# Attention scores computed head by head over 64 array rows, in alternating halves, with pooled keys transposed without zero blocks

## The chip, the core and the metric

The kernel runs on one core of a Trainium2 chip. TensorE (PE in the profile; PEld are its weight loads) does the matrix products, VectorE is DVE, ScalarE is ACT, GpSimd is POOL, and SyncE is SP, which issues the transfers here. The metric is device microseconds of one execution.

## The reference: what is computed

Pooled attention feeds two blocks of dense products. Only the first part is touched by the change. q, k and v have 8 batches, 8 heads, 576 positions and a head width of 64.

```
k_p = k.reshape(B, H, Sp, pool, D).mean(axis=3)       # 576 keys pooled by 8: 72 keys
v_p = v.reshape(B, H, Sp, pool, D).mean(axis=3)
scores = scale * np.matmul(q, k_p.transpose(0, 1, 3, 2))
...
attn = np.exp(scores)
attn = attn / (np.sum(attn, axis=-1, keepdims=True) + 1e-09)
return np.matmul(attn, v_p).astype(np.float32)
...
x = _moe_ref(x=x, **moe_kwargs)        # x @ w_in, softmax-gated, normed, @ w_out
return _moe2_ref(x=x, **moe2_kwargs)   # ((x @ w1) * (x @ w2) @ w3) @ w_out
```

## The kernel before, in words

The work has three stretches. In the first some 145 us the first weights are loaded and converted while attention starts. Up to about 585 us attention and the first dense block run interleaved on PE in slots. From there on the rest of the first block and the second block follow, without attention.

PE and SP follow an order that is written out by hand: each step is `put` into a numbered slot, and the steps of a slot are emitted one after the other, together with a piece of the dense products (`HEAVY`: h is L567, x is L624 to L626). The order on DVE, ACT and POOL in these stretches is set by a scheduler.

Attention works on 16 groups, two for each of the 8 batches; a group has two query tiles of 128 rows, and every second group a third tile of 64, so that there are 40 tiles. For each tile `pq` transposes the queries of the 8 heads, two heads (a pair) at a time, and ACT copies them to `qT`: its 128 rows are two heads of 64. `sc` (L436) computes the scores in two PSUM banks. `exp` takes the maxima on DVE (L454) and the exponentials of 72 keys a head on ACT (L457), `normalize` divides on POOL (L477, L484), `pt` transposes the result, and `av` multiplies it with the pooled values (L539); ACT and DVE copy that away (`split`, L100 and L101, and X, L543).

Three PSUM banks (`bank`, tag "ba", `bufs=3`) are shared in rotation by pq, the two halves of sc, pt, av and the transposed keys (pkm, pkl), so that a step that opens a bank waits until its user three openings earlier has been read.

A batch's pooled keys come into `bdt`, 128 rows by 4 pairs by 2 by 72: for a pair, the two heads' keys stand on the diagonal and zeros elsewhere. One matmul of 128 rows and 144 columns thus gives a pair's scores. The zeros come with the transposes: `pool_k` sums the keys on DVE (L324), ACT spreads the sums into a zeroed `KBD` (L327), and `transpose_k` transposes its four blocks (L358). The last 8 pooled keys (`pool_kl`) are multiplied with a mask into `KLB` on POOL (L346), transposed (L362) and copied by DVE (L368). For the first batch PE itself does the pooling (`pool_k_first`, L340).

An f32 matmul of the program stands in the trace as two weight loads and two matmuls, so a tile's four score matmuls are eight rows of L436. A transpose is one of each, and so are the products of type fp32r.

Of the kernel before, what the change touches and what calls it, by code (L numbers as in the profile page):

```python
# [8 lines left out]
F32 = mybir.dt.float32  # L9
# [3 lines left out]
AF = mybir.ActivationFunctionType  # L13
ALU = mybir.AluOpType
# [4 lines left out]
def attention_moe_kernel(  # L19
# [53 lines left out]
    def bank(name):  # L73
        return PS.tile([P, 512], F32, tag="ba", name=name, bufs=3)
# [7 lines left out]
    ident = const.tile([P, P], F32, tag="ident", name="ident")  # L82
# [50 lines left out]
    def after(d, fn, *args, first=3):  # L133
        put(now + d, fn, *args, first=first)
# [7 lines left out]
    A1 = att.enter_context(tc.tile_pool(name="att1", bufs=1, side="right"))  # L142
    A = att.enter_context(tc.tile_pool(name="att", bufs=2, side="right"))
# [7 lines left out]
    class Rounded:  # L151
        def __init__(self, w, i):
            self.w, self.i = w, i
# [116 lines left out]
    QL = A1.tile([P, H, D], F32, tag="QL", name="QL")  # L270
    KLB = A1.tile([P, H, D], F32, tag="KLB", name="KLB")
    nc.gpsimd.memset(QL, 0.0)
    nc.gpsimd.memset(KLB, 0.0)

    def heads(t, n):
        return t.rearrange("p (o d) -> p o d", o=1).to_broadcast([n, H, D])

    def head_mask(n):
        return mask8[0:n].rearrange("p (h o) -> p h o", o=1).to_broadcast([n, H, D])

    def tree(t, n):

        for w in (4, 2, 1):
            nc.gpsimd.tensor_tensor(t[..., 0 : w * n], t[..., 0 : w * n], t[..., w * n : 2 * w * n], ALU.add)

    class Batch:


        def __init__(self, b):
            self.b = b  # L290
            self.k, self.v = [None, None], [None, None]

        def load_main(self, src, to, i):
            t = A.tile([P, 2, POOL * D], F32, tag="kvn", name=f"kv{self.b}_{i}")
            for hh in range(2):
                nc.sync.dma_start(
                    t[64 * hh : 64 * hh + 64],
                    src[self.b, 4 * i + hh : 4 * i + hh + 3 : 2, 0:512, :].rearrange("h (k e) d -> k h (e d)", e=POOL),
                )
            to[i] = t  # L300

        def load_left(self, src, copies):
            t = A.tile([P, POOL * D], F32, tag="kvl", name=f"kvl{self.b}", bufs=1)
            for c in range(copies):
                nc.sync.dma_start(
                    t[64 * c : 64 * c + 64], src[self.b, :, 512:S, :].rearrange("h (k e) d -> h k (e d)", e=POOL)
                )
            return t

        def load_k(self, i):  # L310
            self.load_main(k, self.k, i)

        def load_kl(self):
            self.kl = self.load_left(k, 1)

        def load_v(self, i):
            self.load_main(v, self.v, i)

        def load_vl(self):
            self.vn = self.load_left(v, 2)  # L320

        def pool_k(self, i):
            kp = A.tile([P, 2, D], F32, tag="kp", name=f"kp{self.b}_{i}", bufs=1)
            nc.vector.tensor_reduce(kp, self.k[i].rearrange("p c (e d) -> p c d e", e=POOL), axis=AX.X, op=ALU.add)  # L324
            for hh in range(2):
                r = slice(64 * hh, 64 * hh + 64)
                nc.scalar.activation(KBD[r, 2 * i : 2 * i + 2, hh, :], kp[r], AF.Copy)  # L327

        def pool_k_first(self, i):

            if i == 0:
                self.pm = bank(f"pkm{self.b}")
                self.bdt = A.tile([P, NP, 2, KP], F32, tag="bdt", name=f"bdt{self.b}")
                nc.gpsimd.memset(self.bdt, 0.0)
            for c in range(2):
                for a in range(2):
                    r, o = slice(D * a, D * a + D), (2 * i + c) * P + D * a
                    for e in range(POOL):
                        s_ = self.k[i][:, c, e * D : e * D + D]
                        nc.tensor.matmul(  # L340
                            self.pm[r, o : o + D], s_, ident[:, r], start=(e == 0), stop=(e == POOL - 1)
                        )

        def pool_kl(self):
            tree(self.kl[0:64], D)
            nc.gpsimd.tensor_tensor(KLB[0:64], heads(self.kl[0:64, 0:D], 64), head_mask(64), ALU.mult)  # L346

        def transpose_k(self):
            if self.b == 0:
                bdt, pm = self.bdt, self.pm.rearrange("p (c a k) -> p c a k", c=NP, a=2)  # L350
                for a in range(2):
                    r = slice(D * a, D * a + D)
                    nc.scalar.activation(bdt[r, :, a, 0:KM], pm[r, :, a, :], AF.Copy)
            else:
                bdt = self.bdt = A.tile([P, NP, 2, KP], F32, tag="bdt", name=f"bdt{self.b}")
                pm = bank(f"pkm{self.b}")
                for p in range(NP):
                    nc.tensor.transpose(pm[:, p * P : p * P + P], KBD[:, p].rearrange("p a d -> p (a d)"), ident)  # L358
                nc.scalar.activation(bdt[:, :, :, 0:KM], pm.rearrange("p (c a k) -> p c a k", c=NP, a=2), AF.Copy)
            pl = bank(f"pkl{self.b}")  # L360
            for p in range(NP):
                nc.tensor.transpose(  # L362
                    pl[:, p * P : p * P + P], KLB[:, 2 * p : 2 * p + 2].rearrange("p a d -> p (a d)"), ident
                )

            def left():
                for p in range(NP):
                    nc.vector.tensor_copy(  # L368
                        bdt[:, p, :, KM:KP],
                        pl[:, p * P + 16 * p : p * P + 16 * p + 16].rearrange("p (a k) -> p a k", a=2),  # L370
                    )

            after(1, left)
# [21 lines left out]
    class Group:  # L395
# [32 lines left out]

        def sc(self, t):
            n, nm = P, f"{self.a}_{t}"  # L430
            qT, bdt = self.st[t], self.batch.bdt
            half = []
            for a in range(2):
# [9 lines left out]
                half.append(sc[0:n, 0 : 4 * KP].rearrange("p (h k) -> p h k", h=4))  # L443
            self.st[t] = half
            after(self.gaps[0], self.exp, t, first=6)

        def exp(self, t):
            n, nm, half = P, f"{self.a}_{t}", self.st[t]
            mx = A.tile([P, H], F32, tag="mx", name="mx" + nm)
            sm = A.tile([P, H], F32, tag="sm", name="sm" + nm)  # L450
            e = A.tile([P, H, KP], F32, tag="ea", name="ea" + nm)
            for a in range(2):
                hs = slice(4 * a, 4 * a + 4)
                nc.vector.tensor_reduce(mx[0:n, hs], half[a], axis=AX.X, op=ALU.max, negate=True)  # L454
                for h in range(4):
                    x = 4 * a + h
                    nc.scalar.activation(  # L457
                        e[0:n, x],
                        half[a][:, h],
                        AF.Exp,  # L460
                        bias=mx[0:n, x : x + 1],
                        scale=1.0,
                        accum_out=sm[0:n, x : x + 1],
                    )
            self.st[t] = e, sm
            after(self.gaps[1], self.normalize, t)
# [243 lines left out]
    for un in units:  # L710
        s_ = SLOTS * un.u
# [49 lines left out]
    with tc.manual_schedule(engines={mybir.EngineType.PE, mybir.EngineType.SP}):  # L761
        for s_ in range(min(events), SLOTS * (NU + 1) + 2):
# [3 lines left out]
            u, c = s_ // SLOTS, s_ % SLOTS  # L766
            kind, n = HEAVY[c], c % 4
# [82 lines left out]
    for m in range(FC):  # L850
# [6 lines left out]
        if m in BLOCKS_AT:  # L857
            i = BLOCKS_AT.index(m)
# [206 lines left out]
```

## Time and profile before

| | |
|---|---|
| median of 3 runs | 1326.9 us (1325.52 to 1329.15) |
| the profiled execution | 1330.36 us, its span 1328.6 us |
| PE busy over the span | 1240.8 us (93%) |
| DVE, ACT, POOL busy | 820.4, 535.9, 421.8 us |
| mean granted PE clock | 0.976 |

Busy time of PE holds the pipelined end of each matmul, so that the pace of a stretch is read from the starts of neighbouring rows and not from the durations.

### The profile page before, as it was taken

How to read it: one execution, taken by the hardware profiler on the slowest of the kernel's cores; microseconds unless marked ns; L12 is line 12 of the kernel's file. 1: busy time of each engine (PE TensorE's matmuls, PEld its weight loads, DVE VectorE, ACT ScalarE, POOL GpSimd, SP SyncE). 2: the span in 40 equal slices, each digit the busy share in tenths (PEclk: the TensorE clock that was granted, in tenths of full speed). 3: DMA queues.
4: the chain of work that ended last, by engine and by line, in shares of the span. 5: the costliest groups of instructions: out<-in, count | busy, mean ns of one | idle time of the engine just before them, and what ended most of it. 6: DMA issues, size and time to landing. Idle time of an engine off the chain costs nothing.

```text
span 1328.6 us, 21980 instructions
## 1 busy us (share of the span) xinstructions
PE 1240.8 (93%) x8284; PEld 1128.1 (85%) x8284; DVE 820.4 (62%) x1627; ACT 535.9 (40%) x1517; POOL 421.8 (32%) x509
## 2 busy tenths in 40 slices
PE   6777999999998999999999999999999999999992
PEld 5466888888888888898898899999999999999992
DVE  4989777777877777644348555545554645454541
ACT  5465666566665656554345222212121212121210
POOL 3433434253434434220000142424242433334220
PEclk8879999999999999999999999999999999999996
DMA  9533445453535464313124101020101101010000
GB/s 233 136 79 104 135 128 159 123 143 116 153 113 140 120 167 120 100 48 126 52 91 153 32 2 64 1 64 1 64 10 55 46 19 64 1 64 1 33 1 32
DMA packets 85698, 109.43 MB, mean 82 GB/s; under 512 B 43608, under 2 KB 43608, under 8 KB 85592
## 3 DMA queue, kind: packets, MB, share of 16 engines
q1 hardware_dynamic: 85592, 108.03, 28.3%
q8 instruction: 65, 1.06, 0.3%
q14 instruction: 41, 0.34, 0.1%
HBM read 78.65 MB, written 29.36 MB: 81 GB/s over the span
## 4 chain that ended last, share of the span: by engine, by line
PE 73%; DVE 11%; DMA 6%; ACT 3%; issue 3%; POOL 1%; SPq 1%; ACTq 0%; DVEq 0%; POOLq 0%
PE p L925 9%; PE p L927 9%; PE p L926 9%; PE h L567 8%; PE acc L971 5%; PE acc L974 5%; PE acc L973 5%; DMA f<-in_moe_w_dram 4%; PE x L625 4%; PE x L626 4%; PE x L624 4%; PE sc L436 2%; PE av L539 2%; PE lt L610 1%; DVE kp L324 1%
## 5 line engine op out<-in xcount | busy, mean ns | idle before, releaser
L945 POOL TENSOR_TENSOR a<-a,b 128x256 f32<-128x256 f32 x72 | 53.0, 736 | 479.4 <-DVE b L944 351.0
L929 ACT ACTIVATE p<-p 128x256 f32<-128x256 f32 x72 | 27.9, 387 | 397.2 <-PE p L927 365.3
L625 PE MATMUL x<-lnl,gwh 128*128 128x256 f32 x576 | 164.1, 285 | 4.1 <-DVE lnl L614 4.0
L624 PE MATMUL x<-lnh,gwh 128*128 128x256 f32 x576 | 167.2, 290 | 0.0
L626 PE MATMUL x<-lnh,gwl 128*128 128x256 f32 x576 | 163.4, 284 | 0.0
L189 POOL TENSOR_TENSOR cvb<-cvb,cvm 128x512 f32<-128x512 f32 x46 | 60.1, 1306 | 212.4 <-DVE cvm L182 159.9
L625 PEld LDWEIGHTS x<-lnl,gwh 128*128 128x128 f32 x576 | 110.7, 192 | 6.1 <-DVE lnl L614 5.2
L974 PE MATMUL acc<-wfl,ph 128*128 128x512 f32 x288 | 113.1, 393 | 0.0
L457 ACT ACTIVATE ea<-sc,mx 128x72 f32<-128x72 f32 x320 | 98.4, 329 | 36.1 <-DVE mx L454 35.9
L973 PE MATMUL acc<-wfh,ph 128*128 128x512 f32 x288 | 112.9, 392 | 0.0
L624 PEld LDWEIGHTS x<-lnh,gwh 128*128 128x128 f32 x576 | 110.6, 192 | 1.2 <-ACT lnh L613 0.2
L626 PEld LDWEIGHTS x<-lnh,gwl 128*128 128x128 f32 x576 | 110.7, 192 | 0.0
L944 DVE TENSOR_TENSOR b<-b,p 128x256 f32<-128x256 f32 x72 | 30.2, 420 | 123.0 <-PE p L927 123.0
L567 PE MATMUL h<-winh,xh 128*128 128x512 f32 x288 | 100.4, 430 | 0.0
L567 PE MATMUL h<-winl,xh 128*128 128x512 f32 x288 | 91.3, 399 | 0.0
L567 PE MATMUL h<-winh,xl 128*128 128x512 f32 x288 | 90.3, 395 | 0.0
L614 DVE TENSOR_TENSOR lnl<-lt,lnh 128x512 fp32r<-128x512 f32 x72 | 49.3, 687 | 55.6 <-ACT lnh L613 55.2
L925 PE MATMUL p<-th,w1h 128*128 128x256 f32 x288 | 81.6, 283 | 1.1 <-ACT p L929 1.1
L971 PE MATMUL acc<-wfh,pl 128*128 128x512 f32 x288 | 82.6, 393 | 0.0
L926 PE MATMUL p<-th,w1h 128*128 128x256 f32 x288 | 81.5, 283 | 0.0
L927 PE MATMUL p<-th,w1l 128*128 128x256 f32 x288 | 81.5, 283 | 0.0
L933 DVE TENSOR_TENSOR u<-p,p 128x256 f32<-128x256 f32 x72 | 30.4, 422 | 77.3 <-PE p L927 77.3
(196 smaller groups left out, 3766.0 us busy)
## 6 DMA issues: line engine op xcount, KB each, us to landing
f<-in_moe_w_dram SPq DMA_DIRECT2D x32, 512.0 KB, 6.2
x2d<-xo SPq DMA_DIRECT2D x36, 256.0 KB, 2.0
xq<-x2d SPq DMA_DIRECT2D x36, 256.0 KB, 2.8
out_dram<-ot SPq DMA_DIRECT2D x36, 256.0 KB, 2.6
kv<-in_k_dram SPq DMA_DIRECT2D x32, 256.0 KB, 3.8
q<-in_q_dram SPq DMA_DIRECT2D x32, 256.0 KB, 7.0
kv<-in_v_dram SPq DMA_DIRECT2D x32, 256.0 KB, 3.7
f<-in_moe_w_out_dram SPq DMA_DIRECT2D x16, 512.0 KB, 5.8
```

The source lines that it names most:

```text
L189: self.engine.tensor_tensor(self.f, self.f, self.m.bitcast(F32), ALU.add)
L457: nc.scalar.activation(e[0:n, x], half[a][:, h], AF.Exp, bias=mx[0:n, x : x + 1], scale=1.0, accum_out=sm[0:n, x : x + 1],)
L567: nc.tensor.matmul(self.ph[:, a], s_[:, c], w_[:, c, a * 512 : a * 512 + 512], start=first, stop=last)
L624: nc.tensor.matmul(o, gw[0][:, f, ws], self.th[:, f], start=(f == 0), stop=False)
L625: nc.tensor.matmul(o, gw[0][:, f, ws], self.tl[:, f], start=False, stop=False)
L626: nc.tensor.matmul(o, gw[1][:, f, ws], self.th[:, f], start=False, stop=(f == FC - 1))
L925: nc.tensor.matmul(o, wh[:, c, fsl], th[:, c], start=c == 0, stop=False)
L926: nc.tensor.matmul(o, wh[:, c, fsl], tl[:, c], start=False, stop=False)
L927: nc.tensor.matmul(o, wl[:, c, fsl], th[:, c], start=False, stop=c == 1)
L971: nc.tensor.matmul(accs[t], pl[:, ts], wh, start=False, stop=(fc == FC - 1))
L973: nc.tensor.matmul(accs[t], ph[:, ts], wh, start=(fc == 0), stop=False)
L974: nc.tensor.matmul(accs[t], ph[:, ts], wl, start=False, stop=False)
```

## The change

The keys of a batch come into one of two tiles `KT`, 128 rows by 4 pairs by 72, with no zeros: the upper 64 rows hold one head of a pair and the lower 64 the other. `sc` does one matmul for each head, 64 rows by 72 columns, alternately for the first head of a pair (rows 0 to 63, first bank) and the second (rows 64 to 127, second bank). The heads of a bank are therefore every second one, and `exp` writes them to their places.

The keys are loaded in another arrangement of heads, so that the pooled sums of two heads stand side by side in `kp`, which is transposed as it is: two transposes in place of four, without KBD and ACT's copies into it. The last 8 keys are summed by POOL into two equal blocks of columns, transposed by one matmul over 64 rows, and copied by two DVE copies in place of four. For the first batch PE pools with 128 moving columns and half as many matmuls. `kl` and `vl` have buffers of their own. Three fills on POOL (KBD, KLB, and `bdt` for the first batch) and the mask product are gone.

```diff
-    KBD = A1.tile([P, NP, 2, D], F32, tag="KBD", name="KBD")
+    KT = [A1.tile([P, NP, KP], F32, tag=f"kt{i}", name=f"kt{i}") for i in range(2)]
-    nc.gpsimd.memset(KBD, 0.0)
-    nc.gpsimd.memset(KLB, 0.0)
...
         def pool_k(self, i):
-            kp = A.tile([P, 2, D], F32, tag="kp", name=f"kp{self.b}_{i}", bufs=1)
+            kp = self.kp[i] = A.tile([P, 2, D], F32, tag="kp", name=f"kp{self.b}_{i}")
             nc.vector.tensor_reduce(kp, self.k[i].rearrange("p c (e d) -> p c d e", e=POOL), axis=AX.X, op=ALU.add)
-            for hh in range(2):
-                r = slice(64 * hh, 64 * hh + 64)
-                nc.scalar.activation(KBD[r, 2 * i : 2 * i + 2, hh, :], kp[r], AF.Copy)
...
         def pool_kl(self):
-            tree(self.kl[0:64], D)
-            nc.gpsimd.tensor_tensor(KLB[0:64], heads(self.kl[0:64, 0:D], 64), head_mask(64), ALU.mult)
+            t = self.kl[0:64]
+            for w in (4, 2):
+                nc.gpsimd.tensor_tensor(t[:, 0 : w * D], t[:, 0 : w * D], t[:, w * D : 2 * w * D], ALU.add)
+
+            for c in (2, 3):
+                nc.gpsimd.tensor_tensor(t[:, c * D : c * D + D], t[:, 0:D], t[:, D : 2 * D], ALU.add)
...
+            if self.b:
+                self.pm = bank(f"pkm{self.b}")
+                for i in range(2):
+                    nc.tensor.transpose(
+                        self.pm[:, i * P : i * P + P], self.kp[i].rearrange("p a d -> p (a d)"), ident
+                    )
+            kt, pm = self.kt, self.pm[:, 0 : NP * KM].rearrange("p (c k) -> p c k", c=NP)
+
+            pl = bank(f"pkl{self.b}")[:, 0:64]
+            nc.tensor.transpose(pl, self.kl[0:64, 2 * D : 4 * D], ident[0:64, 0:64])
+            nc.scalar.activation(kt[:, :, 0:KM], pm, AF.Copy)
...
-            half = []
-            for a in range(2):
-                sc = bank(f"sc{nm}_{a}")
-                for p in range(2):
+            sc = [bank(f"sc{nm}_{a}") for a in range(2)]
+            for p in range(NP):
+                for a in range(2):
+                    r = slice(D * a, D * a + D)
                     nc.tensor.matmul(
-                        sc[0:n, p * 2 * KP : p * 2 * KP + 2 * KP],
-                        qT[:, 2 * a + p, 0:n],
-                        bdt[:, 2 * a + p].rearrange("p a k -> p (a k)"),
-                        start=True,
-                        stop=True,
+                        sc[a][0:n, p * KP : p * KP + KP], qT[r, p, 0:n], kt[r, p], start=True, stop=True
                     )
```

On PE, at the second tile of an odd group, behind `av` and ahead of the x products, this stood before (x2 counts the two pairs of a half; sc_1_0 and sc_1_1 are the two banks):

```order
L539 MATMUL av_3_3397<-ptx_3029,VLL 128x320
L436 MATMUL sc_1_0_3412<-bdt_3183,qT_1_3344 128x144 x2
L436 MATMUL sc_1_1_3415<-bdt_3183,qT_1_3344 128x144 x2
L624 MATMUL x_5_1_3421<-lnh_3080,gwh 128x256
L625 MATMUL x_5_1_3421<-lnl_3081,gwh 128x256
```

And this stands there in the changed kernel (the line numbers are its own; a row is one matmul of the program):

```order
L532 MATMUL av_3_3391<-ptx_3025,VLL 128x320
L434 MATMUL sc_1_0_3406<-kt_105,qT_1_3338 128x72
L434 MATMUL sc_1_1_3407<-kt_105,qT_1_3338 128x72
L434 MATMUL sc_1_0_3406<-kt_105,qT_1_3338 128x72
L434 MATMUL sc_1_1_3407<-kt_105,qT_1_3338 128x72
L434 MATMUL sc_1_0_3406<-kt_105,qT_1_3338 128x72
L434 MATMUL sc_1_1_3407<-kt_105,qT_1_3338 128x72
L434 MATMUL sc_1_0_3406<-kt_105,qT_1_3338 128x72
L434 MATMUL sc_1_1_3407<-kt_105,qT_1_3338 128x72
L617 MATMUL x_5_1_3419<-lnh_3074,gwh 128x256
```

The second bank, which the third matmul of a tile opened before, is now opened by the second matmul of eight; the steps around it are the same.

On DVE, at the same tile, the queue was this before (mx are the two maxima of the tile, one for each bank; xl and X read the banks of av, VBDl are the values of the next batch, ST and e belong to h):

```order
L575 TENSOR_REDUCE ST<-h_1_3312 128x1
L101 TENSOR_TENSOR xl_3353<-av_2_3388,xh_3352 128x256
L543 COPY X_98<-av_2_3388 128x64
L101 TENSOR_TENSOR VBDl<-kv_1_3103,VBDh 64x2x64
L454 TENSOR_REDUCE mx_1_3439<-sc_1_0_3412 128x4
L101 TENSOR_TENSOR VBDl<-kv_1_3103,VBDh 64x2x64
L582 SCALAR_TENSOR_TENSOR e_1_3385,ST<-h_1_3312,e_1_3385 128x1024
L101 TENSOR_TENSOR xl_3353<-av_3_3397,xh_3352 128x256
L543 COPY X_98<-av_3_3397 128x64
L454 TENSOR_REDUCE mx_1_3439<-sc_1_1_3415 128x4
```

In the changed kernel it is this:

```order
L568 TENSOR_REDUCE ST<-h_1_3306 128x1
L101 TENSOR_TENSOR xl_3347<-av_2_3382,xh_3346 128x256
L536 COPY X_98<-av_2_3382 128x64
L101 TENSOR_TENSOR VBDl<-kv_1_3101,VBDh 64x2x64 x2
L180 SCALAR_TENSOR_TENSOR cvb<-f_3366,cvb 128x512
L575 SCALAR_TENSOR_TENSOR e_1_3379,ST<-h_1_3306,e_1_3379 128x1024
L101 TENSOR_TENSOR xl_3347<-av_3_3391,xh_3346 128x256
L536 COPY X_98<-av_3_3391 128x64
L447 TENSOR_REDUCE mx_1_3437<-sc_1_0_3406 128x4
L447 TENSOR_REDUCE mx_1_3437<-sc_1_1_3407 128x4
```

The first maximum has moved behind a weight conversion (cvb), e, xl and X; both maxima now stand together.

On ACT, at the start of the program, the rows up to the first queries were these before:

```order
L170 ACTIVATE cvm<-f_133 128x512
L353 ACTIVATE bdt_164<-pkm_163 64x4x64 x2
L204 ACTIVATE winh<-cvb 128x512
L424 ACTIVATE qT_0_274<-pq_0_269 128x512
L170 ACTIVATE cvm<-f_137 128x512
```

In the changed kernel they are these:

```order
L170 ACTIVATE cvm<-f_131 128x512
L361 ACTIVATE kt_105<-pkm_161 128x4x64
L421 ACTIVATE qT_0_232<-pq_0_227 128x512
L204 ACTIVATE winh<-cvb 128x512
L170 ACTIVATE cvm<-f_135 128x512
```

The queries' copy qT has moved ahead of a weight copy (winh), and the keys take one copy in place of two.

## Rows read from the trace of the kernel before

**Rows 1.** The page: span, and busy time of each engine.

```profile
span 1328.6 us, 21980 instructions
PE 1240.8 (93%) x8284; PEld 1128.1 (85%) x8284; DVE 820.4 (62%) x1627; ACT 535.9 (40%) x1517; POOL 421.8 (32%) x509
```

**Rows 2.** Busy time by stretch (length, engines, granted clock, DMA share, GB/s).

```profile
0.00:145.00 145.00, 107.65 (x604) 85.01 (x604) 115.39 (x230) 74.97 (x244) 60.08 (x83) 0.88 0.55 141
145.00:585.00 440.00, 418.50 (x2863) 383.90 (x2864) 324.15 (x642) 275.49 (x930) 168.79 (x217) 0.99 0.47 128
```

**Rows 3.** Who PE waited for, 145 to 585 us: total, times, longest.

```profile
PE av L539 <- DVE xl L101: 8.5, 5, 1.9
PE sc L436 <- DVE X L543: 7.1, 6, 1.4
...
PE sc L436 <- DVE xl L101: 1.5, 4, 0.4
```

**Rows 4.** The score line, 145 to 585 us: ns min/median/max, first and last start.

```profile
L436 PEld LDWEIGHTS sc<-bdt,qT x248: 186/190/337, 149.9 to 568.4; 128*128 128x128 f32 x124
L436 PE MATMUL sc<-bdt,qT x248: 283/286/607, 150.0 to 568.6; 128*128 128x144 f32 x124
```

**Rows 5.** One tile's scores: in the chain (start, us), and on PE's timeline after idling.

```profile
491.98 0.98 PE sc L436 x8
...
101.61 1.25 PE L436 MATMUL sc<-bdt,qT 128*128 128x144 f32 x8 [0.69 <-ACT qT L424]
102.69 0.49 PE L610 MATMUL lt<-ident,e 128*128 128x128 f32 x3
```

**Rows 6.** A tile that waits for its second bank, timelines of PE and DVE.

```profile
384.98 0.65 PE L436 MATMUL sc<-bdt,qT 128*128 128x144 f32 x4
386.69 0.73 PE L436 MATMUL sc<-bdt,qT 128*128 128x144 f32 x4 [1.06 <-DVE X L543]
...
386.34 0.21 DVE L543 COPY X<-av 128x64 f32<-128x64 f32 x1
```

**Rows 7.** PE's timeline where matmuls use 64 of the array's columns, and leave them.

```profile
12.73 1.15 PE L340 MATMUL pkm<-ident,kv 128*64 128x64 f32 x20
...
15.41 0.46 PE L340 MATMUL pkm<-ident,kv 128*64 128x64 f32 x5
15.79 0.66 PE L362 MATMUL pkl<-ident,KLB 128*128 128x128 f32 x4
16.28 0.60 PE L421 MATMUL pq<-ident,q 128*128 128x128 f32 x4
```

**Rows 8.** L340 by shape, 13 to 15.5 us: busy us, mean ns.

```profile
L340 PE MATMUL pkm<-ident,kv 128*64 128x64 f32 x56 | 2.9, 225 | 0.0
L340 PEld LDWEIGHTS pkm<-ident,kv 128*64 128x64 f32 x54 | 2.7, 138 | 0.0
```

**Rows 9.** PE's timeline at four transposes that run back to back.

```profile
290.44 0.60 PE L610 MATMUL lt<-ident,e 128*128 128x128 f32 x4
290.87 1.15 PE L436 MATMUL sc<-bdt,qT 128*128 128x144 f32 x8
```

**Rows 10.** ACT's copies into KBD: by line, and what ACT waited for (0 to 590 us).

```profile
L327 ACT ACTIVATE KBD<-kp 64x128 f32<-64x128 f32 x28 | 8.6, 309 | 26.8 <-DVE kp L324 26.6
...
ACT KBD L327 <- DVE kp L324: 26.6, 14, 3.1
```

**Rows 11.** ACT's and PE's timeline at the first scores.

```profile
15.96 0.77 ACT L353 ACTIVATE bdt<-pkm 64x256 f32<-64x256 f32 x2 [1.83 <-PE pkm L340]
16.75 0.63 ACT L204 ACTIVATE winh<-cvb 128x512 fp32r<-128x512 f32 x1
17.41 0.60 ACT L424 ACTIVATE qT<-pq 128x512 f32<-128x512 f32 x1
...
18.06 0.64 PE L436 MATMUL sc<-bdt,qT 128*128 128x144 f32 x3 [1.17 <-ACT qT L424]
```

**Rows 12.** From the tile of rows 6 on: its normalization on POOL, its transposes on PE.

```profile
394.17 0.55 POOL L484 TENSOR_TENSOR pr<-ea,sm 128x64 f32<-128x64 f32 x2
...
397.63 0.60 PE L502 MATMUL pt<-ident,pr 128*128 128x128 f32 x4
398.07 0.27 PE L505 MATMUL px<-ident,pr 128*128 128x128 f32 x1
```

More of the change, by code (lines that the diff above doesn't have):

```diff
@@ L290, in __init__, with load_main, load_left @@
             self.b = b
-            self.k, self.v = [None, None], [None, None]
-        def load_main(self, src, to, i):
+            self.k, self.v, self.kp = [None, None], [None, None], [None, None]
+            self.kt = KT[b % 2]
+        def load_main(self, src, to, i, heads_of):
             t = A.tile([P, 2, POOL * D], F32, tag="kvn", name=f"kv{self.b}_{i}")
-            for hh in range(2):
+            for r in range(2):
                 nc.sync.dma_start(
-                    t[64 * hh : 64 * hh + 64],
-                    src[self.b, 4 * i + hh : 4 * i + hh + 3 : 2, 0:512, :].rearrange("h (k e) d -> k h (e d)", e=POOL),
+                    t[64 * r : 64 * r + 64],
+                    src[self.b, heads_of(4 * i, r), 0:512, :].rearrange("h (k e) d -> k h (e d)", e=POOL),
                 )
             to[i] = t
-        def load_left(self, src, copies):
-            t = A.tile([P, POOL * D], F32, tag="kvl", name=f"kvl{self.b}", bufs=1)
+        def load_left(self, src, copies, tag):
+            t = A.tile([P, POOL * D], F32, tag=tag, name=f"{tag}{self.b}", bufs=1)
             for c in range(copies):
@@ L310, in load_k @@
         def load_k(self, i):
-            self.load_main(k, self.k, i)
+            self.load_main(k, self.k, i, lambda h, r: slice(h + 2 * r, h + 2 * r + 2))
         def load_kl(self):
-            self.kl = self.load_left(k, 1)
+            self.kl = self.load_left(k, 1, "kl")
         def load_v(self, i):
-            self.load_main(v, self.v, i)
+            self.load_main(v, self.v, i, lambda h, r: slice(h + r, h + r + 3, 2))
         def load_vl(self):
-            self.vn = self.load_left(v, 2)
+            self.vn = self.load_left(v, 2, "vl")
         def pool_k(self, i):
-            kp = A.tile([P, 2, D], F32, tag="kp", name=f"kp{self.b}_{i}", bufs=1)
+            kp = self.kp[i] = A.tile([P, 2, D], F32, tag="kp", name=f"kp{self.b}_{i}")
             nc.vector.tensor_reduce(kp, self.k[i].rearrange("p c (e d) -> p c d e", e=POOL), axis=AX.X, op=ALU.add)
-            for hh in range(2):
-                r = slice(64 * hh, 64 * hh + 64)
-                nc.scalar.activation(KBD[r, 2 * i : 2 * i + 2, hh, :], kp[r], AF.Copy)
         def pool_k_first(self, i):
@@ L332, in pool_k_first @@
                 self.pm = bank(f"pkm{self.b}")
-                self.bdt = A.tile([P, NP, 2, KP], F32, tag="bdt", name=f"bdt{self.b}")
-                nc.gpsimd.memset(self.bdt, 0.0)
-            for c in range(2):
-                for a in range(2):
[L337 to L342, printed above, removed]
@@ L344, in pool_kl @@
-        def pool_kl(self):
-            tree(self.kl[0:64], D)
-            nc.gpsimd.tensor_tensor(KLB[0:64], heads(self.kl[0:64, 0:D], 64), head_mask(64), ALU.mult)
-        def transpose_k(self):
-            if self.b == 0:
-                bdt, pm = self.bdt, self.pm.rearrange("p (c a k) -> p c a k", c=NP, a=2)
+            for a in range(2):
+                for e in range(POOL):
+                    nc.tensor.matmul(
+                        self.pm[D * a : D * a + D, i * P : i * P + P],
+                        self.k[i][:, a, e * D : e * D + D],
+                        ident,
+                        start=(e == 0),
+                        stop=(e == POOL - 1),
+                    )
@@ L351, in transpose_k @@
                 for a in range(2):
                     r = slice(D * a, D * a + D)
[L353 to L367, printed above, removed]
                     nc.vector.tensor_copy(
-                        bdt[:, p, :, KM:KP],
-                        pl[:, p * P + 16 * p : p * P + 16 * p + 16].rearrange("p (a k) -> p a k", a=2),
+                        kt[r, :, KM:KP], pl[r].rearrange("p (c a k) -> p c a k", c=NP, a=2)[:, :, a]
@@ L430, in sc @@
             n, nm = P, f"{self.a}_{t}"
-            qT, bdt = self.st[t], self.batch.bdt
-            half = []
-            for a in range(2):
-                sc = bank(f"sc{nm}_{a}")
-                for p in range(2):
-                    nc.tensor.matmul(
-                        sc[0:n, p * 2 * KP : p * 2 * KP + 2 * KP],
-                        qT[:, 2 * a + p, 0:n],
-                        bdt[:, 2 * a + p].rearrange("p a k -> p (a k)"),
-                        start=True,
-                        stop=True,
-                    )
-                half.append(sc[0:n, 0 : 4 * KP].rearrange("p (h k) -> p h k", h=4))
-            self.st[t] = half
+            qT, kt = self.st[t], self.batch.kt
+            sc = [bank(f"sc{nm}_{a}") for a in range(2)]
+            for p in range(NP):
+                for a in range(2):
+                    r = slice(D * a, D * a + D)
+                    nc.tensor.matmul(
+                        sc[a][0:n, p * KP : p * KP + KP], qT[r, p, 0:n], kt[r, p], start=True, stop=True
+                    )
+            self.st[t] = [x[0:n, 0 : NP * KP].rearrange("p (h k) -> p h k", h=NP) for x in sc]
             after(self.gaps[0], self.exp, t, first=6)
@@ L455, in exp @@
                 for h in range(4):
-                    x = 4 * a + h
+                    x = 2 * h + a
                     nc.scalar.activation(
@@ L460, in exp @@
                         AF.Exp,
-                        bias=mx[0:n, x : x + 1],
+                        bias=mx[0:n, 4 * a + h : 4 * a + h + 1],
                         scale=1.0,
```

3 lines of the change are left out of this document (2 added, 1 removed).

## The prediction

> **What bounds the kernel now.** I read the busy times first. PE is busy for 1240.8 of 1328.6 us, and no other engine for more than 62% [rows 1]. By stretch, PE idles 37 of the first 145 us, but only 21.5 of the 440 us from 145 to 585 us [rows 2], where 31 of the 40 tiles have their scores (248 rows, eight a tile) [rows 4]. So in the first stretch PE mostly waits for others, and what it does there costs little. In the second each added 0.1 us of PE work is 0.1 us of time. Then I read who PE waits for in the second: xl and X, DVE's reads of the banks of av. That is five waits in av itself, 8.5 us, and ten in sc, 8.6 us [rows 3]. These ten are the second half of a tile's scores, waiting for its bank: in the tile at 384.98 us the first four rows run, DVE reads X at 386.34, and the other four start at 386.69 [rows 6].
>
> **The scores: pace inside.** A tile takes 0.98 us in a full stream [rows 5], 0.123 us for each of eight rows of 144 columns. Half as many columns should need half of that, 0.06 us. But a program matmul still needs two weight loads of 128 columns, and there are twice as many matmuls: 16 loads a tile in place of 8. The trace gives a load's length only with its latency: 190 ns for 128 columns [rows 4] and 138 ns for 64 [rows 8]. The difference, 52 ns for 64 columns, makes 0.104 us for 128, which is an estimate from these two rows. So the loads set the pace, not the columns. If loads into the upper and the lower half of the rows run side by side, a tile needs eight in a row, 0.83 us, and nothing near half of 0.98. If not, it needs sixteen, 1.66 us. No row here uses halves of the array's rows. The nearest uses halves of its columns: L340 does 16 rows in one half and then 16 in the other. Within a half they begin 0.06 us apart (five in 0.46 us, the last of them 0.22 long), but over a change of halves 20 begin within 0.93 us, 0.049 apart [rows 7, 8]. So rows of both halves ran side by side. I take eight in a row, and keep sixteen as the bound.
>
> **The scores: the edges.** When PE leaves the halves, something is lost. The last row of pkm begins at 15.41 + 4 x 0.06 = 15.65 us, and pkl, which is done with all columns, begins 0.15 us later where 0.06 is the pace: 0.09 us of emptying. Its own load is then not hidden either (four of its transposes take 0.49 us to the next, where 0.43 is the pace) [rows 7, 9]. For a load of f32 scores that exposed part is 0.10 us: after idling, a tile takes 1.08 us to the next step instead of 0.98 [rows 5]. I take it that 64-row matmuls among 128-row ones pay the same at both edges. The bound below is nothing, if only a change of columns empties the array.
>
> The Trainium skill, TensorEngine Tiling (Array Packing), section Key Properties, states that changing the tiling mode, not just the tile, drains TensorE, which speaks against this change 80 times over. The trace agrees for the one change of mode that it has, 0.09 us in [rows 7], and shows none between 128 and 64 rows. By that rule both edges are paid, which is the sum below; without it the sum is that of the first rival. The skill's TensorE: Matmul & The Clock Gate, section LDWEIGHTS, has a load's time go by its columns whatever the rows, 107 ns for 128; with it in place of 0.104 the sum below grows by 0.7 us.
>
> **A plain tile** is then 0.09 (emptying) + 8 x 0.104 + 0.06 (the last columns) + 0.09 + 0.10 (the next step's load) = 1.17 us, 0.19 more than 0.98. There are 21 in the second stretch: +4.0 us.
>
> **A tile that waits for its bank** loses more. Before, half of it ran ahead of the wait, and 0.10 + 4 x 0.123 = 0.59 us came behind. Now the second matmul of eight opens the second bank, and everything behind it on PE waits too. DVE's queue up to X is as before, so the bank comes free at the same distance from av. Behind it come all loads of the lower half, 0.83 + 0.06 + 0.09 + 0.10 = 1.08 us: +0.49 us. There are ten: +4.9 us.
>
> **The transposes.** KBD's four become two: -0.22 us at 0.108 each [rows 9]. pkl's four become one over 64 rows: -0.43 + 0.06, and two edges of 0.14 and 0.19 us, together -0.04. Six batches lie in the second stretch: -1.6 us.
>
> **The start.** ACT copies the keys once instead of twice, which saves about half of 0.77 us, and qT moves ahead of winh, 0.63 us. The first scores wait for qT [rows 11], so they come 1.0 us earlier. ACT then has winh still to do, so I count half: -0.5 us. The first batch's pooling has the same columns in half as many rows, and the keys' transfers keep size and order: nothing.
>
> **ACT, DVE, POOL.** The 28 copies into KBD go, 8.6 us, and with them 26.6 us in which ACT stood before them waiting for kp [rows 10]. In the second stretch ACT idles 165 of 440 us and PE never waits for these copies, so I count nothing there. Behind kp on DVE stand the xl that PE does wait for, and kp stays. DVE's two fewer key copies and POOL's product are hidden the same way. The maxima are late next: on the tile of rows 6 the first one moves behind cvb, e, xl and X, some 2.9 us. Its normalization ended at 394.72 and the last transpose started at 398.07, so 3.4 us cover it, barely [rows 12]. If that cover is gone, a wait of up to 1 us at seven such tiles is added. In the first stretch, the nine tiles' edges fall into PE's idle time; ACT's relief and the later maxima there pull against each other, and I take nothing, with 3 us to either side.
>
> **Sum:** 4.0 + 4.9 - 1.6 - 0.5 = +6.8 us. On the profiled execution's 1330.4 us that is 1337.2. The median of the runs is 3.5 us below it, so I forecast 1326.9 + 6.8 = 1333.7, rounded 1334 us.
>
> **Rival 1: the edges are free**, because only a change of columns empties the array. Then the next loads are hidden, and a plain tile takes 0.83 us: 21 x -0.15 = -3.2. Tiles with a bank wait still lose 0.10 + 0.83 - 0.59 = 0.34, ten times: +3.4. The transposes give -0.59 x 6 = -3.6, the start -0.5: -3.9 us, 1323. This is the case on the other side, not slower. It decides from the point where an edge costs under about 0.1 us instead of 0.19. For it: no row shows this edge. Against it: [rows 7] show the other one.
>
> **Rival 2: loads into the two halves follow each other.** Then a plain tile takes 1.66 + 0.34 = 2.0 us, +1.0, and one with a wait about +1.1: 21 + 11 - 2 = +30 us, 1357. Against it speaks L340's overlap [rows 7]; for it, that those were other halves.
>
> **Rival 3: ACT's relief reaches PE in the first stretch.** A KBD wait is 1.9 us in the mean [rows 10]; batches 1 and 2, with two each, are pooled ahead of 145 us. If PE waits behind ACT for all of these, 7.6 us come back, and the sum is -0.8 us, 1326; with cheap edges as well it is near 1316. For it: PE idles 37 us there. Against it: ACT idles 70 of those 145 us, and DVE is busy for 115 [rows 2].
>
> **How the numbers follow.** The forecast has 0.55, rival 1 0.20, rival 2 0.10, rival 3 0.15. The forecast's own range is 1329 to 1340: emptying from 0.04 to 0.09 at an edge, the late maxima, and 3 us of the first stretch. Leaving out rival 2 above, and the cheap end of rival 3 below, gives 1317 to 1343. Within 0.3%, 4 us either way, is about what a measurement here can tell from no change. Faster by more: most of rival 3's half with cheap edges, not quite half of rival 1, a little of the forecast: 0.24. Within: half of rival 1, the rest of rival 3, the low end of the forecast: 0.22. Slower: 0.54.
>
> **What would show it.** Score rows should begin in pairs, one from each half, with about 0.105 us between pairs; 0.06 or 0.21 would prove the pace wrong. The step behind a tile's last score should begin about 0.15 us or more after it, and the tile should take 1.1 to 1.2 us. Waits of sc for X and xl should stay at ten or so in the second stretch, with more work behind them. The second stretch should be longer by some 7 us and the third by nothing. I am wrong if an edge is free, if the loads are not side by side, or if the first stretch moves by more than 3 us.

## The result, and the profile after

The changed kernel takes 1345.28 us (median of 4 runs, 1342.91 to 1349.61), the one before 1326.21 us (4 runs, 1322.95 to 1329.15). The ratio is 1.0139 (1.0112 to 1.0165), +19 us: slower, as forecast, but by more than the +6.8 us of the sum, and 2 us above the range. The profiled run took 1344.70 us. Its page begins so (span; busy time of each engine):

```profile
span 1342.9 us, 22350 instructions
PE 1255.9 (94%) x8502; PEld 1134.7 (84%) x8502; DVE 819.5 (61%) x1611; ACT 526.1 (39%) x1488; POOL 414.9 (31%) x506
```

PE is busy for 15.1 us more [rows 1]. Busy time in the second stretch, in the columns of [rows 2]:

```profile
145.00:585.00 440.00, 421.79 (x2968) 379.12 (x2966) 311.84 (x609) 257.59 (x871) 157.19 (x209) 0.96 0.45 125
```

The column to look at is the granted clock of the second stretch, 0.96 where it was 0.99. The score line there (ns min/median/max, first and last start):

```profile
L434 PEld LDWEIGHTS sc<-kt,qT x496: 182/188/335, 147.6 to 584.7; 64*128 64x128 f32 x166
L434 PE MATMUL sc<-kt,qT x496: 272/272/486, 147.6 to 584.7; 64*128 64x72 f32 x166
```

These are the same 31 tiles, now of 16 rows. From the start of the first row to the start of the last they take 437.1 us, where they took 418.6 [rows 4]: +18.5 us. The first stretch is 2.4 us shorter (147.6 against 150.0), what follows the last score 1.8 us shorter (758.2 against 760.0 to the end of the span). So the whole loss lies in the second stretch (the two profiles differ by 14.3 us, less than the medians, since the profiled execution before was longer than its four runs). It is not in PE's waits there (total us, times, longest):

```profile
PE av L532 <- DVE xl L101: 8.4, 5, 1.8
PE sc L434 <- DVE X L536: 6.6, 6, 1.5
PE sc L434 <- DVE xl L101: 2.1, 5, 0.5
```

sc waits eleven times and 8.7 us, where it was ten times and 8.6; av waits as before [rows 3]. The work between the waits has become longer. A plain tile on PE's timeline:

```profile
354.39 1.11 PE L434 MATMUL sc<-kt,qT 64*128 64x72 f32 x16
355.44 0.39 PE L617 MATMUL x<-lnh,gwh 128*128 128x256 f32 x1
355.66 0.28 PE L618 MATMUL x<-lnl,gwh 128*128 128x256 f32 x1
```

The rows of the stream of x begin 0.12 us apart, so the first x row would have stood at 355.54 without an edge: 1.15 us from the first score row to the step behind. A tile that waits for its second bank:

```profile
316.27 0.44 PE L434 MATMUL sc<-kt,qT 64*128 64x72 f32 x2
317.62 1.08 PE L434 MATMUL sc<-kt,qT 64*128 64x72 f32 x14 [0.91 <-DVE X L536]
318.63 0.39 PE L617 MATMUL x<-lnh,gwh 128*128 128x256 f32 x1
318.85 0.28 PE L618 MATMUL x<-lnl,gwh 128*128 128x256 f32 x1
```

Only two rows run ahead of the wait (it was four [rows 6]), and 318.85 - 0.12 - 317.62 = 1.11 us come behind it. DVE's way to that bank, and the same tile before on PE and DVE:

```profile
315.66 1.23 DVE L568 TENSOR_REDUCE ST<-h 128x1 f32<-128x1024 f32 x1
316.92 0.42 DVE L101 TENSOR_TENSOR xl<-av,xh 128x256 fp32r<-128x256 f32 x1
```

```profile
316.77 0.65 PE L436 MATMUL sc<-bdt,qT 128*128 128x144 f32 x4
318.48 0.73 PE L436 MATMUL sc<-bdt,qT 128*128 128x144 f32 x4 [1.06 <-DVE X L543]
319.16 0.28 PE L625 MATMUL x<-lnl,gwh 128*128 128x256 f32 x1
...
316.52 1.23 DVE L575 TENSOR_REDUCE ST<-h 128x1 f32<-128x1024 f32 x1
317.77 0.43 DVE L101 TENSOR_TENSOR xl<-av,xh 128x256 fp32r<-128x256 f32 x1
```

The second half started 1.71 us behind the first row before and starts 1.35 us behind it now. DVE goes to xl straight from ST in both traces, so here its own queue sets when the bank comes free, not av. The transposed keys, in the changed kernel:

```profile
154.79 0.38 PE L354 MATMUL pkm<-ident,kp 128*128 128x128 f32 x2
155.10 0.27 PE L360 MATMUL pkl<-ident,kl 64*128 64x64 f32 x1
155.31 0.73 PE L560 MATMUL h<-winh,xh 128*128 128x512 f32 x2
```

Up to here all is near the forecast. The rest shows in a tile that waits in av and again in sc, PE's timeline at 343 us:

```profile
342.33 0.38 PE L532 MATMUL av<-pth,VBDh 128*128 128x256 f32 x1 [1.36 <-DVE xl L101]
...
343.12 0.44 PE L434 MATMUL sc<-kt,qT 64*128 64x72 f32 x2
344.05 1.65 PE L434 MATMUL sc<-kt,qT 64*128 64x72 f32 x14 [0.50 <-DVE xl L101]
345.63 1.22 PE L560 MATMUL h<-winh,xh 128*128 128x512 f32 x2
...
350.92 0.77 PE L418 MATMUL pq<-ident,q 128*128 128x128 f32 x4
```

The same place in the kernel before:

```profile
342.56 0.38 PE L539 MATMUL av<-pth,VBDh 128*128 128x256 f32 x1 [1.29 <-DVE xl L101]
...
344.29 0.76 PE L436 MATMUL sc<-bdt,qT 128*128 128x144 f32 x4 [0.37 <-DVE xl L101]
344.79 0.71 PE L567 MATMUL h<-winh,xh 128*128 128x512 f32 x2
...
347.65 0.60 PE L421 MATMUL pq<-ident,q 128*128 128x128 f32 x4
```

The waits are nearly the same. But the same six pairs of h take 5.29 us (345.63 to 350.92) instead of 2.86 (344.79 to 347.65): they run at half the clock. All stretches of the second part in which the trace of the changed kernel has the clock at its lower level, 1.2 GHz:

```profile
201.10:207.90 6.80, 6.45 (x26) 5.25 (x27) 3.25 (x8) 2.87 (x17) 2.05 (x2) 0.50 0.93 262
344.40:351.20 6.80, 6.80 (x26) 5.40 (x25) 3.08 (x5) 2.54 (x16) 2.16 (x4) 0.50 1.08 269
392.20:395.60 3.40, 3.40 (x18) 3.40 (x17) 3.34 (x8) 2.25 (x10) 0.00 (x0) 0.50 0.00 0
419.50:426.30 6.80, 6.80 (x27) 5.40 (x26) 3.08 (x5) 2.53 (x16) 2.22 (x4) 0.50 1.06 245
467.30:470.70 3.40, 3.40 (x18) 3.40 (x18) 3.37 (x9) 2.20 (x9) 0.00 (x0) 0.50 0.00 0
494.60:501.40 6.80, 6.53 (x26) 5.35 (x26) 3.01 (x8) 2.92 (x17) 1.92 (x2) 0.50 0.94 238
542.40:545.80 3.40, 3.40 (x22) 3.27 (x20) 3.37 (x9) 1.68 (x5) 0.00 (x0) 0.50 0.00 0
```

And in the trace of the kernel before:

```profile
274.40:277.80 3.40, 3.04 (x9) 2.66 (x10) 1.46 (x4) 2.44 (x17) 1.26 (x1) 0.50 0.80 219
482.60:486.00 3.40, 3.40 (x14) 3.40 (x15) 2.52 (x7) 2.01 (x7) 1.26 (x1) 0.50 0.32 104
```

That is 37.4 us at half clock in place of 6.8. Each of the seven begins within 4 us of the start of a tile that waits for its second bank, four of them with a wait in av just ahead. It is not a matter of one run: the mean granted clock of the whole span was 0.963 to 0.968 in the four runs after, and 0.973 to 0.983 in the 41 runs of the kernel before that stand beside the experiments. As the lower level is one half, what is missing to 1, doubled and multiplied by the span, estimates the time at half clock in the whole span: 91 us after and 60 before, in the mean of the runs, so 31 us more, as in the two profiles.

### The profile page after: what moved, and what is told of

Same layout as the page of the kernel before. It is cut to its first block, busy times and chain, and to the rows that moved or that the text cites. A ratio compares the mean times of both kernels' runs of the same rounds, so it can differ in the third digit from the quotient of the medians.

```text
span 1342.9 us, 22350 instructions
## 1 busy us (share of the span) xinstructions
PE 1255.9 (94%) x8502; PEld 1134.7 (84%) x8502; DVE 819.5 (61%) x1611; ACT 526.1 (39%) x1488; POOL 414.9 (31%) x506
## 4 chain that ended last, share of the span: by engine, by line
PE 73%; DVE 13%; DMA 5%; ACT 3%; issue 3%; POOL 1%; SPq 0%; DVEq 0%; ACTq 0%; POOLq 0%
PE h L560 9%; PE p L918 9%; PE p L920 9%; PE p L919 9%; PE acc L964 5%; PE acc L967 5%; PE acc L966 5%; PE x L617 4%; PE x L618 4%; PE x L619 4%; DMA f<-in_moe_w_dram 3%; PE sc L434 2%; DVE cvb L180 1%; PE av L532 1%; DVE ST L568 1%
## 5 line engine op out<-in xcount | busy, mean ns | idle before, releaser
L560 PE MATMUL h<-winh,xh 128*128 128x512 f32 x288 | 103.6, 443 | 0.0
L560 PE MATMUL h<-winl,xh 128*128 128x512 f32 x288 | 94.1, 409 | 0.0
L434 PE MATMUL sc<-kt,qT 64*128 64x72 f32 x640 | 56.5, 303 | 23.1 <-ACT qT L421 9.7
```

Source lines behind the costliest of these rows:

```text
L434: nc.tensor.matmul(sc[a][0:n, p * KP : p * KP + KP], qT[r, p, 0:n], kt[r, p], start=True, stop=True)
L560: nc.tensor.matmul(self.ph[:, a], s_[:, c], w_[:, c, a * 512 : a * 512 + 512], start=first, stop=last)
```

## The experiments

**The theories.** A: the loss is in the scores, some 8 us from the edges and the later bank as forecast, and some 11 us from the clock. C: the scores are near the forecast, and the rest comes from the other half of the change, the keys' path and the new order on DVE and ACT. Within A, two sources of the clock: A1, PE's idle time at the wait for the second bank; A2, the 64-row matmuls themselves, or the waits in av, whatever the bank does. The kernel before took 1327.73 us in the first four comparisons (median of 19 runs) and 1327.2 in the last four (22 runs).

**1. The keys' path alone** (e1_keys_only). The new transposes and copies stay; the scores are those of before, 128 rows by 144 columns, from two tiles whose zeros are written once.

```diff
-    KT = [A1.tile([P, NP, KP], F32, tag=f"kt{i}", name=f"kt{i}") for i in range(2)]
+    BDT = [A1.tile([P, NP, 2, KP], F32, tag=f"bdt{i}", name=f"bdt{i}") for i in range(2)]
+    for t_ in BDT:
+        nc.gpsimd.memset(t_, 0.0)
...
-                        sc[a][0:n, p * KP : p * KP + KP], qT[r, p, 0:n], kt[r, p], start=True, stop=True
+                        sc[0:n, p * 2 * KP : p * 2 * KP + 2 * KP],
+                        qT[:, 2 * a + p, 0:n],
+                        bdt[:, 2 * a + p].rearrange("p a k -> p (a k)"),
...
```

> The keys' new path alone (pooled sums transposed as they are, last keys through one 64-row transpose, no fills or copies for KBD and KLB), with the scores as before: 128 rows, 144 columns, zeros on the diagonal. Theory A (the loss is made by the scores over half the rows: their edges and later bank, some 8 us, and half clock that comes with them, some 11 us): the second stretch is as long as before or 1 to 3 us shorter, TensorE's clock falls there no more often than before (two spells), and the time is 1319 to 1326 us. Rival theory C (the loss comes from the new order on DVE and ACT and the keys' path): it stays above 1335 us.

Measured: 1324.37 us (1321.49 to 1329.2), ratio 0.9974 (0.9957 to 0.9991). The score rows go from 149.1 to 566.8, 417.7 us, with 10.2 us at half clock. That is three stretches of half clock where I had expected two. C falls as far as the keys' path goes: it costs nothing and even gains a little. The 21 us between this kernel and the changed one come with the scores. Kernel 1 does not settle the new order on DVE, since its first maximum stands where it stood before; kernel 5 has the later maxima.

**2. One half after the other** (e2_half_by_half). The same eight matmuls, the four of the upper rows first.

```diff
-            for p in range(NP):
-                for a in range(2):
+            for a in range(2):
+                for p in range(NP):
```

> The changed kernel with a tile's four matmuls of the upper rows first and then the four of the lower, instead of in turn; nothing else. If loads set the pace and run side by side only for alternating halves, a tile needs some 13 loads in a row in place of 8, 1.6 us in place of 1.05, and the second bank is opened later: 1355 to 1362 us in all. If the columns set the pace (0.06 us a row), or the halves did not run side by side anyway, the tile takes about as long as in the changed kernel and the time stays at 1345 us or falls by the 3 us of the later bank.

Measured: 1348.03 us, ratio 1.0156 (1.0129 to 1.0184). A plain tile, and one behind a wait in av, on PE's timeline:

```profile
361.08 1.62 PE L434 MATMUL sc<-kt,qT 64*128 64x72 f32 x16
362.62 0.39 PE L617 MATMUL x<-lnh,gwh 128*128 128x256 f32 x1
...
205.05 2.92 PE L434 MATMUL sc<-kt,qT 64*128 64x72 f32 x16
207.90 1.22 PE L560 MATMUL h<-winh,xh 128*128 128x512 f32 x2
```

A tile takes 1.54 us in place of 1.05, 0.49 more, which for 31 tiles would be 15 us. The waits for the second bank are nearly gone, since it is now the fifth matmul that opens it: 1.3 us, four times, in place of 8.7. The first tile behind an av wait still falls to half clock without any bank wait (205.05: 2.85 us). There are 23.8 us at half clock. My 1355 and more was too high: the later opening gives the waits back, 7 us, and this profile has 13.6 us less at half clock in the second stretch. All four of its stretches follow a wait in av.

**3. Rows to fill the wait** (e3_filler). Six or ten matmuls of 128 rows by 224 columns, whose results nobody reads, stand ahead of the scores of each tile that waits, so that PE works until the bank is free.

```diff
             sc = [bank(f"sc{nm}_{a}") for a in range(2)]
+            if self.a > 0 and t == 1 - self.a % 2:
+                for _ in range(10 if t else 6):
+                    nc.tensor.matmul(sc[0][:, 288:512], negid, win[0][:, 0, 0:224], start=True, stop=True)
```

> The changed kernel with products that nobody reads (128 rows, 224 columns, into free columns of the first score bank) ahead of the tiles that wait for their second bank: 6 for the shorter wait, 10 for the longer one, 0.6 and 1.1 us that PE otherwise idles. They shorten no wait. Theory A1 (the clock falls because of PE's idle time around the bank wait): the half-clock spells after these tiles go, and 4 to 10 us come back, 1335 to 1341 us. Rival A2 (it falls because 64-row matmuls themselves count as little work, or because of the idle time in av): as many spells as in the changed kernel, 1343 to 1348 us.

Measured: 1348.18 us, ratio 1.0153 (1.0121 to 1.0185). By the total it decides nothing: the first stretch is 12 us longer (second stretch from 159.8 us on). The second stretch went the way of A1, 428.8 us for the 31 tiles in place of 437.1, with 13.6 us at half clock.

**4. The same scores, later** (e4_late_scores). The scores of the tiles that wait are put behind the dense products of their slot, the exponentials move with them, and the normalization follows one slot sooner, so that the transposes stay in their slot.

```diff
...
-            put(base + 2 + 4 * t, grp.sc, t)
+            late = a > 0 and t == 1 - a % 2
+            put(base + 2 + 4 * t + late, grp.sc, t, first=0 if late else 5)
```

> The changed kernel with the scores of the tiles that wait for their second bank put behind the slot's dense products, so that their bank is free when they come; the transposes of their results stay in their slot. Both theories: the waits of sc for X and xl go, 8 us. A1 (clock falls because of idle time at the bank wait): the half-clock spells go too, another 5 to 10 us: 1326 to 1333 us. A2 (64-row matmuls themselves, or the idle time in av): the spells stay, 1336 to 1340 us.

Measured: 1321.55 us (1315.86 to 1327.61), ratio 0.9956 (0.9931 to 0.998), which is more than even A1 had promised. PE's timeline at a wait in av, and its waits from 145 to 585 us:

```profile
339.92 0.39 PE L533 MATMUL av<-pth,VBDh 128*128 128x256 f32 x1 [1.47 <-DVE xl L101]
...
340.62 0.62 PE L561 MATMUL h<-winh,xh 128*128 128x512 f32 x2
...
342.08 1.11 PE L434 MATMUL sc<-kt,qT 64*128 64x72 f32 x16
```

```profile
PE av L533 <- DVE xl L101: 8.2, 5, 1.8
PE pt L496 <- DVE X L537: 3.5, 6, 0.8
```

av waits as long as ever, but dense products of 128 rows follow it. sc waits no more; 3.5 of its 8.7 us have gone to pt. Half clock: one stretch of 3.4 us, at 202 us. The 31 tiles take 415.0 us, 22 less, with the same 64-row matmuls. So neither 64-row matmuls in themselves nor the waits in av in themselves hold the clock down.

**5. The early second bank with full rows** (e7_early_bank). Kernel 1, but its four matmuls a tile alternate between the banks, so that the second of four opens the second bank, as in the change.

```diff
-            for a in range(2):
-                sc = bank(f"sc{nm}_{a}")
-                for p in range(2):
+            sc = [bank(f"sc{nm}_{a}") for a in range(2)]
+            for p in range(2):
+                for a in range(2):
```

> The new keys' path with scores over 128 rows and 144 columns as before, but with the two banks in turn: the second bank is opened by a tile's second matmul instead of its third. No matmul over half the rows is left but the last keys' transpose. If the later second bank and PE's idle time behind it bring the half clock (A1), the second stretch gets several more half-clock spells than the 3 of the keys' path alone, and the time is 1332 to 1340 us. If it takes matmuls over half the rows (A2), only the wait itself costs, ten times 0.25 us: 3 spells as before, and 1325 to 1329 us.

Measured: 1334.09 us (1327.91 to 1334.82), ratio 1.0048 (1.0029 to 1.0067); 420.9 us for the tiles. Its waits from 145 to 585 us:

```profile
PE sc L436 <- DVE X L542: 9.3, 6, 1.6
PE av L538 <- DVE xl L101: 8.7, 5, 2.0
PE sc L436 <- DVE xl L101: 2.5, 4, 0.6
```

sc waits 11.8 us, more than in the change, and yet there are only 13.6 us at half clock, four stretches where kernel 1 has three. The time lies in A1's range, but the half clock is nearer to A2. The order on DVE is that of the change too, both maxima late. So the early opening and that order cost some 10 us against kernel 1, of which the second stretch of the two profiles shows 3; the other 11 us up to the changed kernel come with the 64-row matmuls. The bank's wait does not bring the 37.4 us.

**6. Filling in the second stretch alone** (e3b_filler_second). As 3, from the third batch on (`self.a > 3`).

> The changed kernel with the fillers of the earlier run (128 rows, unread, into free columns of the first score bank, ahead of tiles that wait for their second bank) from the third batch on alone, since in the first stretch they delayed the attention itself by 12 us. In that run the second stretch had 14 us of half clock instead of 38 and was 8 us shorter. If the idle time at the bank wait brings the half clock (A1), this gives 1334 to 1340 us in all with at most 3 spells; if not (A2), 1343 to 1348 us.

Measured: 1337.45 us (1332.86 to 1341.38), ratio 1.0079 (1.0052 to 1.0106). PE's timeline behind a wait in av:

```profile
345.80 0.39 PE L535 MATMUL av<-pth,VBDh 128*128 128x256 f32 x1 [1.72 <-DVE xl L101]
...
346.50 0.83 PE L433 MATMUL sc<-winh,negid 128*128 128x224 f32 x6
347.25 1.38 PE L437 MATMUL sc<-kt,qT 64*128 64x72 f32 x16
```

With full rows between the wait and the 64-row scores, this profile has no half clock at all in the second stretch, and the tiles take 422.4 us: useless work was added, and 14.7 us were gained. (This profile is the fastest of seven runs; their mean clocks were 0.970 to 0.980. By the medians 7.8 us were gained.) The time is what A1 had forecast, but the filling rows also stand between the wait in av and the 64-row scores, so this run does not tell the two waits apart.

**7 and 8. Kernel 1, and the kernel before, with the late scores** (e5_keys_late, e6_before_late). The edit of 4 on each.

> The keys' new path with scores over 128 rows, and the tiles that waited for their bank put behind the slot's dense products. Beside the changed kernel with the same late scores (1321.6 us) it differs only in the scores over half the rows. If their edges cost 0.19 us a tile and nothing else is left of them, it is 6 us faster in the second stretch: 1313 to 1318 us in all. If halves cost nothing once the wait is gone, both are equal, 1320 to 1323 us.

> The kernel before with the tiles that waited for their bank put behind the slot's dense products, nothing else. The ten waits of sc, 8.6 us, go: 1317 to 1320 us, if no other wait takes their place; 1324 to 1327 us if one does. Against the keys' path with the same late scores it tells what the keys' path is worth by itself, 1 to 4 us by the first runs.

Measured: kernel 7 takes 1315.49 us (1312.2 to 1319.52), ratio 0.9913 (0.9878 to 0.9948), the best of all and faster than both kernels; kernel 8 takes 1323.49 us (1320.94 to 1329.01), ratio 0.9984 (0.9963 to 1.0004). So the gain of 4 is not that of the late order alone: on full rows, where the clock was not lost, the order gives 4 us (before; its interval includes no change) and 9 us (keys), on 64 rows 24. In the profiles of 7 and 8 that gain stands in the first stretch: the second begins at 144.3 and 143.9 us in place of 149.1 and 150.0, and is itself at most 1.3 us shorter, since other waits, above all of pt (6.1 and 5.8 us), took the place of those of sc. For kernel 8 I had 1324 to 1327 us in that case. With the late order the halves still cost 1321.55 - 1315.49 = 6 us, as I had forecast from their edges, but the intervals of the two ratios overlap, and the place is another: in the two profiles the second stretch is no longer with halves (415.0 against 416.4 us), since PE waits less in it (13.7 against 19.2 us in all) and loses the clock for 3.4 us instead of 10.2. It begins 3.6 us later (147.9 against 144.3).

The second stretch side by side, one profile each (the 31 tiles from first to last start; half clock in it; waits of sc), and the mean clock of the whole span in all runs of a kernel:

| kernel | tiles, us | half clock, us | sc waits, us | clock, all runs |
|---|---|---|---|---|
| before | 418.6 | 6.8 | 8.6 | 0.973 to 0.983 |
| after | 437.1 | 37.4 | 8.7 | 0.963 to 0.968 |
| 1 keys alone | 417.7 | 10.2 | 9.2 | 0.974 to 0.980 |
| 2 half by half | 437.3 | 23.8 | 1.3 | 0.966 to 0.971 |
| 3 filled everywhere | 428.8 | 13.6 | 1.0 | 0.967 to 0.972 |
| 4 late scores | 415.0 | 3.4 | none | 0.974 to 0.982 |
| 5 early bank, full rows | 420.9 | 13.6 | 11.8 | 0.971 to 0.977 |
| 6 filled, second stretch | 422.4 | none | 0.7 | 0.970 to 0.980 |
| 7 keys, late | 416.4 | 10.2 | none | 0.978 to 0.981 |
| 8 before, late | 419.2 | 3.4 | none | 0.976 to 0.983 |

A1 and A2 each fall as the whole story. The bank wait without 64-row scores has 13.6 us at half clock (5), 64-row scores straight behind av with hardly a bank wait 23.8 (2), both together 37.4. Dense products between av's wait and the 64-row scores bring the clock back to where it was before (4), and a few full rows there bring back part of it (3), in one profile all (6). So it is the combination that costs: a wait, and 64-row scores right behind it. A difference of one or two stretches between single profiles says little. Over the whole span, by the mean clocks of all runs and as estimated above, it is 60 us at half clock before, 61 in kernel 1, 70 in 5, 86 in 2, 91 in the changed kernel and 61 in 4. By that the 64-row scores matter most, and what the bank wait adds between 2 and the changed kernel is not shown. Why these scores lose the clock where full ones mostly don't (fewer rows at work, or a tile that takes longer) was not separated.

## Why the prediction was right in its direction and too small

- **The pace: right.** Score rows begin in pairs, one from each half, 6 or 7 ns apart, and the pairs 112 ns apart (160 after the first), where I had 0.105. Rival 2 is out as long as the order alternates; in kernel 2, where four of one half follow four of the other, a tile takes 1.54 us, between the two.
- **The edges: right.** From the row before to the first score row it is 202 ns behind lt, 209 behind x, 239 behind av and 319 behind h, where it was 109, 118, 151 and 230: +0.09 each time. A plain tile is 0.09 + 1.15 = 1.24 us where I had 1.17, +0.26 over [rows 5]. Rival 1 is out.
- **The tile that waits: half right.** 1.11 us behind the wait where I had 1.08. Before it was 0.56 (at 318.48 us, counted the same way), so +0.55 for +0.49. But I took the bank to come free at the same distance from av. Ahead of h it does (1.15 us behind av's last row in both traces), and such a tile costs 0.56 us more. Ahead of x it came 0.3 to 0.6 us nearer to av in four of six tiles, and the one at 316 us costs only 0.28 us more in all (2.78 to 3.06 us from av's last row to the fourth row of x). That fits DVE's queue setting the time there, as shown above: what a plain tile ahead has added then only shortens the wait.
- **The transposes: right.** From pkm's first row to h's second it is 0.85 us, and it was 1.11 in the same count (366 us): six times -0.26 is -1.5, I had -1.6.
- **ACT, DVE, POOL: right.** PE waits for no later maximum in the second stretch; pt is not among its waits.
- **The start: too cautious.** The first scores begin at 16.64 us, 1.4 earlier than in [rows 11] (I had 1.0, half counted), and the first stretch is 2.4 us shorter, a third of what rival 3 asked.
- **The step that failed** is the premise from which all of this was added up: "In the second each added 0.1 us of PE work is 0.1 us of time", and with it "the second stretch should be longer by some 7 us". Each piece was priced at the clock of the trace before, and the sum has no term for a change of the clock itself. The pieces as now measured, between the starts of the first and the last tile, are 18 plain tiles at 0.26, six tiles ahead of h at 0.56, six ahead of x with some 2.0 together (two of them estimated), and -1.5 for the transposes: 8.6 us. PE's waits outside these tiles are 2.2 us shorter. That leaves 6.4 of the 18.5 us.

The rest, 12 us, is the clock: 30.6 us more at 1.2 GHz, 0.40 of each. Two other readings agree. Six pairs of h lose 2.43 of 5.29 us at half clock, 0.46 of each; kernel 6 gets back 14.7 us for 37.4, 0.39 of each, with the filling rows still in it. That makes 12 to 14 us, and with the 6.4 some 18 to 20, where 18.5 were measured. The traces show it without any price too. Of the 30 sections from one tile's start to the next, eight have half clock in one trace or the other; these are 17.4 us longer together, and the 22 others 1.2 us. The Trainium skill, TensorE: Matmul & The Clock Gate, section Terms, prices throttled time at the share of pulses left out, here one half; by that the clock is 15.3 us, an estimate, and the runs show somewhat less.

The warning was on the page of before: in its second stretch the mean clock is 0.99 and not 1 [rows 2], which is two stretches at half clock, and both stand at a wait of av with scores right behind. The second, on PE:

```profile
482.57 0.58 PE L539 MATMUL av<-pth,VBDh 128*128 128x256 f32 x1 [1.94 <-DVE xl L101]
...
483.81 2.12 PE L436 MATMUL sc<-bdt,qT 128*128 128x144 f32 x8
```

This one began at 482.60 us, as av resumed and ahead of its scores, so there a wait with full rows around it was enough. The change thinned the very work that follows these waits. The Trainium skill, the same page, section A second HAM failure mode: psum-queue depth-cycling, tells of a kernel whose clock went up and down because PE paused briefly between groups of matmuls as it cycled through its PSUM banks. This case agrees in part: pauses of 0.3 to 2 us for banks stand ahead of every fall in the two traces, but with full rows behind them (kernel 5) they brought 13.6 us and not 37.4. It would have been a rival, and I didn't weigh it.

## What to carry to other kernels

Price a change to TensorE's work by its rows, and then ask which waits it stands next to: here the work behind a wait went with whether the clock held, and that was worth more than all the edges together. When a step waits for a bank, try first to move the step behind other dense work: that took 24 us off the changed kernel without touching its matmuls. On full rows the same move gave 4 and 9 us. Halving the rows of these f32 products halved neither a tile's time (1.24 us for 0.98) nor its loads (16 rows where there were 8); it paid nothing here, and what gain there was came with the keys' path (3 us alone, 8 us under the late order).

## What the hardware showed unexpectedly

- Two f32 matmuls of 64 rows in the two halves of the array's rows begin 6 to 7 ns apart. Four of one half followed by four of the other overlap only in part at the change: 1.34 us from the first row's start to the sixteenth's in the tile at 361 us, where eight pairs take 0.84 and sixteen rows one after the other, 112 ns apart, would take 1.68.
- Going from 128 to 64 rows costs 0.09 us whatever stood before, the same as the change of columns in [rows 7].
- At waits of av and sc that leave 1.2 to 2.2 us from one row's start to the next the clock went to half for 3.4 or 6.8 us in some tiles and not in others of the same kernel. Which tile it hits was not explained.
